# Modulation rows in 32-column strips, an eleventh leading block, and stores on another queue, in an adaLN + spectral mixer + MLP kernel

## The chip, the cores and the metric

One core of a Trainium2 chip runs the whole program in one launch. The metric is the device time of one execution in microseconds (us). Engines are named as in the profile: PE (TensorE, the matrix engine; PEld is its weight load), DVE (VectorE), ACT (ScalarE), POOL (GpSimd) and SP (SyncE, here only a queue that issues DMAs). An engine works through its own instructions in one order, which is fixed when the program is built.

## The reference

The reference is a forward pass and its vector-Jacobian product: the output, and the gradients of ten inputs (`out_1` to `out_9` after the output `out_0`; `B_x` is held constant). Cut to what matters:

```python
mod = (silu(c) @ w_mod).reshape(1, 6, 1, 1024)      # six rows: sa, ca, ga, sb, cb, gb
h = layernorm(x) * (1 + ca) + sa
x = x + ga * irfft2(rfft2(h) * (w_r + 1j * w_i))     # 2048 tokens x 1024
h = layernorm(x) * (1 + cb) + sb
x = x + gb * (gelu(layernorm(h) @ w1 + b1) @ w2 + b2)   # w1 1024x3584, w2 3584x1024
out, vjp = jax.vjp(f, A_x, A_w_r, A_w_i, B_w1, B_b1, B_w2, B_b2, c, w_mod)
return out, *vjp(grad_out)
```

The six modulation rows each need a product of one row of 1024 values with 1024x1024 weights. `out_9` is the gradient of `w_mod`: the outer product of silu(c) with the six row gradients, 1024x6144 values in bfloat16.

## The kernel before

Data are bfloat16, sums float32 in PSUM. Tokens are handled in four blocks of 512 (`NB`), the 3584 hidden columns in 28 blocks of 128 (`NFC`). The stages, in order of time:

1. *Start* (0 to 122 us). Modulation rows, layer norm of x, the turned gradient `gBoT` = (gb * grad_out)^T, and the products `ph = w2^T gBoT`, one block of 128 hidden columns at a time (`ph_part`: for each of four token blocks `j` a sum of eight matmuls into a PSUM tile of the pool "f", which has four buffers). `ph_out` casts each sum into one of four `phs` slots and, at the fourth, stores the slot to `d_ph` from POOL's queue. Beside this DVE scales and folds the normed x (`fold_d`, `fold_pair`, `fold_tok`) into `fbuf`.
2. *Spectral stage* (`spectral_core`, from `s_fwd` on), the transforms as products with cosine and sine matrices, then `consume_fwd` for each token block: residual, two layer norms, and the normed rows `n3`. The `ph` blocks that were not computed at the start are written behind it in the program, and fill PE where it waits.
3. *MLP*: `z_block` (product with w1, then GELU and its derivative on ACT and DVE) and `bo_pass` (product with w2), in the order of the list `plan`. The GELU buffers `gts` alternate between two sets, so a z block's casts wait for the product `hh` of the block two before it.
4. *Backward*: gradients through w1, the layer norms and the spectral part, with the products of the w2 gradient (`gw2_product`) and the w1 gradient (`pieces`, `gw1_quads`) handed out one at a time by `fill`.

*The modulation rows.* `u_b` holds silu(c) with each value repeated over 128 columns, so a product with a weight block gives the row already repeated in all 128 partitions. `mod_block(r, h)` does one half row (512 columns): one 1 MB load (`mod_load`) from SP's queue, eight matmuls, and a cast into its place by `nc.any` (the builder chooses DVE or ACT). The weight tiles `wblk` come from a ring of three buffers. Rows 5 and 1 come first; row 0 (two halves) stands behind block 3, and rows 2, 3 and 4 (six halves, three each) behind blocks 5 and 7. Row 0 is then multiplied by 8 and folded; 1 is added to rows 1 and 4.

*The order.* `ordered()` keeps a matmul behind the PE instruction written before it; `tc.issue_after(ins)` does the same for another engine. `tc.high_priority()` marks an instruction as urgent, which lets the builder put it ahead of others that are ready. `PH_EARLY = 10` says that blocks 0 to 10 are computed at the start; `load_w2t(fc)` loads a transposed w2 block into a ring of four, and `load_w1` starts the w1 loads at block 14 and block 27.

*The gradient of w_mod.* For rows 4, 2, 1 and 0 the last stage runs two generators beside the last products: `gmod_chain` (DVE: loads of `w_mod`, a product and a sum) and `gmod_scaled`, 32 scalings on ACT of a broadcast row `gr` into a ring of five buffers `gw`, each stored by a 256 KB DMA from POOL's queue. The loop at the end of the kernel draws one scaling per piece of the w1 gradient, and two for each of the last nine pieces. The last pieces are `gw1_quads`, four rounds of seven sums in which ACT copies ("snap") a partial sum out of PSUM before the next product is added to it:

```python
        for _ in range(2 if n >= left - 9 else 1):
            next(scaled, None)
```

Of the kernel before, what the change touches and what calls it, by code (L numbers as in the profile page):

```python
# [14 lines left out]
ALU = mybir.AluOpType  # L15
AX = mybir.AxisListType

P = 128
S = 2048
D = 1024  # L20
F = 3584
NT = S // P
NDC = D // P
NFC = F // P
KH = D // 2
# [10 lines left out]
def kernel(  # L36
# [24 lines left out]
    nc = tc.nc  # L61
# [11 lines left out]
    def ps_s(name):  # L73
        return psum.tile([P, 512], FP32, tag="s", name=name)
# [7 lines left out]
    ones_bf = const.tile([P, P], BF16, name="ones_bf")  # L82
# [168 lines left out]
    sarx = reg.tile([P, 3 * D], BF16, name="sar", tag="gm")  # L251
    sar = sarx[:, 0:2 * D].rearrange("p (a c d) -> p a c d", a=2, c=1)
# [5 lines left out]
    u_b = small.tile([P, NDC, P], BF16, name="u_b", tag="gmrow", bufs=1)  # L258
# [3 lines left out]
    sb_row, saf = sb_saf[:, 0, :], sb_saf[:, 1, :]  # L262
    MOD_DST = {0: sar[:, 0, 0, :], 1: opca_row, 2: ga_row, 3: sb_row, 4: opcb_row, 5: gb_row}
    wring = [0]

    def mod_tile():
        wring[0] += 1
        return reg.tile([P, NDC, KH], BF16, name="wblk", tag=PXT[3 + wring[0] % 3])

    def mod_load(r, h, wblk, eng, parts=1):  # L270
        cb = 2 * r + h
        src = w_mod[:, cb * KH:(cb + 1) * KH].rearrange("(j p) n -> p j n", p=P)
        for k in range(parts):
            js = slice(k * NDC // parts, (k + 1) * NDC // parts)
            eng.dma_start(out=wblk[:, js, :], in_=src[:, js, :])

    def mod_block(r, h, wblk=None):
        if wblk is None:
            wblk = mod_tile()[:]
            mod_load(r, h, wblk, nc.sync)  # L280
        pm = (ps_s, ps_d)[wring[0] % 2]("pm")
        for jc in range(NDC):
            nc.tensor.matmul(pm[:], lhsT=u_b[:, jc, :], rhs=wblk[:, jc, :], start=(jc == 0), stop=(jc == NDC - 1))
        dst = MOD_DST[r][:, h * KH:(h + 1) * KH]
        with tc.high_priority():
            nc.any.tensor_copy(out=dst, in_=pm[:])
        if r in (1, 4):
            nc.vector.tensor_scalar(out=dst, in0=dst, scalar1=1.0, scalar2=None, op0=ALU.add)

    def fold_d(dst, src, tmp):  # L290
        n = src.shape[1]
        fwd = src.rearrange("p c (b w) -> p c b w", w=512)[:, :, :, 0:256]
        rev = bass.AP(tensor=src.tensor, offset=src.offset + 1023, ap=[src.ap[0], [D, n], [-512, 2], [-1, 256]])
        tv = tmp.rearrange("p c (s b w) -> p c s b w", s=2, w=256)
        tt(tv[:, :, 0], fwd, rev, ALU.add)
        tt(tv[:, :, 1], fwd, rev, ALU.subtract)
        dv = dst.rearrange("p c (a b w) -> p c a b w", b=2, w=256)
        tt(dv[:, :, :, 0, :], tv[:, :, :, 0, :], tv[:, :, :, 1, :], ALU.add)
        return tt(dv[:, :, :, 1, :], tv[:, :, :, 0, :], tv[:, :, :, 1, :], ALU.subtract)
# [226 lines left out]
    last_pe = [None]  # L526

    def ordered():
        return tc.issue_after(last_pe[0].ins)

    PH_EARLY, PH_KEEP = 10, NFC - 4

    def ph_out(fc, j, pp):
        ph2 = phs[fc % 4]
# [9 lines left out]
    def ph_part(fc, js):  # L544
        for j in js:
            pp = ps_f("pp")
            for cch in range(NDC):
                last_pe[0] = nc.tensor.matmul(pp[:], lhsT=wt[:, fc % 4, cch, :], rhs=gBoT[j][:, cch, :],  # L548
                                              start=(cch == 0), stop=(cch == NDC - 1))
            ph_out(fc, j, pp)  # L550
# [24 lines left out]
    for j in range(4):  # L575
        n = 0
# [351 lines left out]

    phs.append(reg.tile([P, 4, BW], BF16, name="phr", tag="ph")[:])

    late_mods = [(r, h) for r in (2, 3, 4) for h in range(2)]
    for fc in range(PH_EARLY):
        if fc > 1:
            ph_part(fc, (0, 1, 2, 3))
        load_w2t(fc + 4)
        if fc == 4:
            with ordered():
                small_rows()
        if fc == 3:
            for h in range(2):  # L940
                with ordered():
                    mod_block(0, h)
            nc.vector.tensor_scalar(out=sar[:, 0], in0=sar[:, 0], scalar1=8.0, scalar2=None, op0=ALU.mult)
            fold_d(saf.rearrange("p (c d) -> p c d", c=1), sar[:, 0], sar[:, 1])
        if fc in (5, 7):
            with ordered():
                for r, h in late_mods[3 * (fc // 2 - 2):3 * (fc // 2 - 1)]:
                    mod_block(r, h)

    ph_part(PH_EARLY, (0, 1, 2, 3))  # L950
    early_pe = last_pe[0]
# [51 lines left out]
    def load_w1(n):  # L1003
        for _ in range(n):
            g = len(w1s)
            wtile = reg.tile([P, NDC, BW], BF16, name=f"w1_{g}", tag=W1T[g])
            with tc.issue_after(w2t_in[0].ins):
                w1_in.append(nc.sync.dma_start(out=wtile[:], in_=w1_v[:, :, g * BW:(g + 1) * BW]))
            w1s.append(wtile)
# [3 lines left out]
    for fc in range(PH_EARLY + 1, NFC):  # L1013
        if fc >= PH_EARLY + 4:
            load_w2t(fc)
            load_w1({14: 2, 27: 5}.get(fc, 0))
        if fc == N3_AT:
            n3Ts = [reg.tile([P, NDC, BW], BF16, name="n3Ta", tag="uv3")]
        for js in ((0, 1), (2, 3)) if fc < PH_KEEP else ((0, 1),):
            ph_part(fc, js)  # L1020
            if n3Ts and n3_turned[0] < NDC:
                cch = n3_turned[0]
                n3_turned[0] += 1
                pt = (ps_s, ps_d)[cch % 2]("pn")
                for q in range(4):
                    with ordered():
                        last_pn = nc.tensor.matmul(pt[:, q * P:(q + 1) * P], lhsT=n3h[0][:, q, cch * P:(cch + 1) * P], rhs=ident,
                                                   start=True, stop=True)
                last_pe[0] = last_pn
                with tc.high_priority():  # L1030
                    (s_copy, dve_copy)[cch % 2](n3Ts[0][:, cch, :], pt[:])
# [261 lines left out]
    def gmod_scaled(rows):  # L1293
        for n in range(len(rows) * NDC):
            k, jc = n // NDC, n % NDC
            gw, r = w1g["gw"][n % 5], rows[k]
            with tc.issue_after(w1g["ev"].ins):
                nc.scalar.activation(out=gw, in_=w1g["gr"][k], func=ACT.Identity, scale=u_rt[:, jc:jc + 1])
            nc.gpsimd.dma_start(out=out_9[jc * P:(jc + 1) * P, r * D:(r + 1) * D], in_=gw)
            yield  # L1300

    step_in = []
# [556 lines left out]
    for n in range(left):  # L1859
        fill(1)  # L1860
        k = [(32 - CHAIN_EARLY) * min(max(n + 17 + j - left, 0), 14) // 14 for j in range(2)]
        for _ in range(k[1] - k[0]):
            with tc.issue_after(w1g["dve"].ins):
                next(chain)
        for _ in range(2 if n >= left - 9 else 1):
            next(scaled, None)
    fin2 = reg.tile([P, 2, P], BF16, name="fin2", tag="ph")
    make_identity(nc, fin2[:, 0, :])
# [41 lines left out]
```

## Time and profile before

| | |
|---|---|
| median of 3 runs | 1374.16 us (1373.96 to 1374.2) |
| profiled execution | 1372.29 us |
| span of its profile, first to last instruction | 1370.3 us |
| granted TensorE clock, mean | 0.997 |
| PE, DVE, ACT, POOL busy | 98%, 79%, 58%, 28% of the span |
| DMA | 330 MB, 241 GB/s on the mean |

How to read the rows that follow. A timeline row is: start, duration (us), engine, line of the kernel, operation, output<-inputs by the program's names, tile and shape, and xN for N instructions merged; in brackets the idle time of the engine just before, and what released it. Durations of merged rows overlap at their ends, so the cost of a group is read from its start to the next group's start. A window row is: stretch, its length, then busy us of PE, PEld, DVE, ACT and POOL (instructions in brackets), granted clock, busy share of the DMA engines, GB/s. In a wait row stand the total, the number of times and the longest.

### The profile page before, as it was taken

What the parts mean: (1) busy time and instruction counts of PE and PEld (TensorE: products, weight loads), DVE (VectorE), ACT (ScalarE), POOL (GpSimd) and SP (SyncE); (2) the same over time, 40 slices, a digit from 0 to 9 for tenths busy, and PEclk for the clock granted to TensorE, in tenths of its full rate; (3) what the DMA queues carried; (4) which work ended last, traced back from release to release, by engine and by line L of the source; (5) the groups of instructions that cost most, each with busy time, mean ns of one, the idle gap of its engine ahead of it and who ended that gap; (6) DMA issues with size and microseconds to landing.
All of it is one profiled execution on the core that took longest, in us unless ns stands there. A gap on an engine that the chain in (4) does not pass through costs nothing. (4 is left out here: it accounts for less than half of the span.)

```text
span 1370.3 us, 18631 instructions
## 1 busy us (share of the span) xinstructions
PE 1345.6 (98%) x6899; PEld 651.0 (48%) x6899; DVE 1077.2 (79%) x1467; ACT 792.4 (58%) x1120; POOL 390.3 (28%) x436
## 2 busy tenths in 40 slices
PE   7999999999999999999999999999999999999997
PEld 4445566444444444444444444444644555444443
DVE  6997889999988878787620578889888488976985
ACT  4864667767877765665414593445732554544456
POOL 6273642411112122212211010112344330332163
PEclk9999999999999999999999999999999999999999
DMA  9975594899787887698999699988579878899876
GB/s 326 322 196 140 160 256 154 250 279 318 262 254 252 212 261 246 199 289 233 284 278 224 181 217 311 296 254 257 179 238 270 222 160 237 207 245 251 201 271 244
DMA packets 356401, 330.08 MB, mean 241 GB/s; under 512 B 203866, under 2 KB 298736, under 8 KB 356182
## 3 DMA queue, kind: packets, MB, share of 16 engines
q1 hardware_dynamic: 314310, 201.02, 57.2%
q0 software_dynamic: 35232, 120.00, 26.0%
q10 hardware_dynamic: 6768, 7.87, 1.7%
q8 instruction: 54, 0.88, 0.3%
q14 instruction: 37, 0.30, 0.1%
HBM read 165.73 MB, written 114.87 MB: 205 GB/s over the span
## 5 line engine op out<-in xcount | busy, mean ns | idle before, releaser
L1230 PE MATMUL pg<-w1T,gzr 128*128 128x512 bf16 x896 | 195.8, 380 | 0.0
L548 PE MATMUL pp<-gBoT,wt 128*128 128x512 bf16 x832 | 185.4, 379 | 3.2 <-ACT pho L540 1.9
L1076 PEld LDWEIGHTS <-w 128*128 128x128 bf16 x896 | 87.2, 98 | 107.4 <-issue 2.9
L1230 PEld LDWEIGHTS <-gzr 128*128 128x128 bf16 x896 | 86.5, 98 | 108.5 <-issue 5.8
L548 PEld LDWEIGHTS <-wt 128*128 128x128 bf16 x832 | 81.0, 98 | 97.9 <-issue 5.3
L1770 PE MATMUL gw1acc<-gzh,n3n 128*128 128x512 bf16 x512 | 111.8, 380 | 0.0
L1076 PE MATMUL pz<-n3Ta,w 128*128 128x512 bf16 x448 | 98.8, 380 | 1.4 <-ACT gt L1079 1.4
L1076 PE MATMUL pz<-n3Tb,w 128*128 128x512 bf16 x448 | 99.0, 380 | 0.0
L1770 PEld LDWEIGHTS <-n3n 128*128 128x128 bf16 x640 | 62.3, 98 | 76.7 <-issue 3.1
L195 DVE TENSOR_TENSOR ct<-ct 128x2048 bf16<-128x2048 bf16 (+1 forms) x84 | 91.5, 1120 | 4.3 <-ACT n L514 2.0
L1079 ACT ACTIVATE gt<-pz,b_col 128x512 bf16<-128x512 f32 x112 | 72.8, 682 | 37.3 <-PE pz L1076 33.1
L1130 PEld LDWEIGHTS <-hhA 128*128 128x128 bf16 x608 | 58.9, 98 | 73.2 <-issue 3.0
L1087 ACT ACTIVATE gt<-gt 128x2048 bf16<-128x2048 bf16 x28 | 53.5, 1911 | 58.3 <-DVE gt L195 58.3
L1411 PE MATMUL gw2acc<-gB,hhsA 128*128 128x512 bf16 x384 | 84.8, 380 | 0.0
L195 DVE TENSOR_TENSOR gt<-gt,gt 128x2048 bf16<-128x2048 bf16 x56 | 68.4, 1223 | 17.7 <-ACT gt L1089 16.8
L1419 ACT CAST gwo<-gw2acc 128x512 bf16<-128x512 f32 x40 | 23.5, 588 | 87.5 <-PE gw2acc L1411 84.2
L1411 PEld LDWEIGHTS <-hhsA 128*128 128x128 bf16 x384 | 37.5, 98 | 43.5
L1083 ACT ACTIVATE gt<-gt 128x2048 bf16<-128x2048 bf16 x28 | 53.4, 1908 | 3.1 <-DVE hhC L195 2.4
L540 ACT CAST pho<-pp 128x512 bf16<-128x512 f32 x68 | 38.6, 584 | 27.3 <-PE pp L548 24.1
L1774 ACT CAST gwo<-gw1acc 128x512 bf16<-128x512 f32 x40 | 23.0, 579 | 53.6 <-PE gw1acc L1770 41.6
L1089 ACT ACTIVATE gt<-gt 128x2048 bf16<-128x2048 bf16 x28 | 53.3, 1905 | 0.3
L1411 PE MATMUL gw2acc<-gB,otl 128*128 128x512 bf16 x224 | 50.0, 380 | 0.0
(414 smaller groups left out, 2710.3 us busy)
## 6 DMA issues: line engine op xcount, KB each, us to landing
gzr<-d_gz SPq DMA_DIRECT2D x28, 512.0 KB
d_ph<-pho POOLq DMA_DIRECT2D x21, 512.0 KB, 5.5
wblk<-in_w_mod_dram SPq DMA_DIRECT2D x10, 1024.0 KB
out_dram<-otl POOLq DMA_DIRECT2D x40, 256.0 KB, 4.1
d_hh<-hhA POOLq DMA_DIRECT2D x19, 512.0 KB, 5.6
wrw<-in_w_mod_dram SPq DMA_DIRECT2D x32, 256.0 KB
w<-in_B_w_dram SPq DMA_DIRECT2D x7, 1024.0 KB
hhC<-d_ph SPq DMA_DIRECT2D x14, 512.0 KB
```

The lines of the kernel that those rows point to most:

```text
L195: return nc.vector.tensor_tensor(out=out, in0=a, in1=b, op=op)
L540: copy(out=ov, in_=pv)
L548: last_pe[0] = nc.tensor.matmul(pp[:], lhsT=wt[:, fc % 4, cch, :], rhs=gBoT[j][:, cch, :], start=(cch == 0), stop=(cch == NDC - 1))
L1076: last_pe[0] = nc.tensor.matmul(pz[:], lhsT=w1s[g][:, cch, k * P:(k + 1) * P], rhs=n3T[:, cch, :], start=(cch == 0), stop=(cch == NDC - 1))
L1079: z_in = nc.scalar.activation(out=zb[:, k, :], in_=pz[:], func=ACT.Identity, bias=b1_col[:, fc:fc + 1], scale=1.0)
L1083: nc.scalar.activation(out=av, in_=zb, func=ACT.Square)
L1087: nc.scalar.activation(out=sg, in_=bv, func=ACT.Sigmoid, scale=2.0 * GK)
L1089: nc.scalar.activation(out=bv, in_=bv, func=ACT.Sigmoid, scale=-2.0 * GK)
L1130: last_pe[0] = nc.tensor.matmul(pbs[i][:], lhsT=hh[:, k, i * P:(i + 1) * P], rhs=wp[:, k, :], start=False, stop=(g == 6 and k == 3))
L1230: last_pg[0] = nc.tensor.matmul(pgs[i][:], lhsT=gzs[b, g][:, k, i * P:(i + 1) * P], rhs=w1Ts[g][:, k, h * KH:(h + 1) * KH], start=(g == 0 ...
L1411: nc.tensor.matmul(acc[:], lhsT=hh_of(fc)[:, t, :], rhs=gBs[t // 4][:, t % 4, h * KH:(h + 1) * KH], start=(t == 0), stop=(t == NT - 1))
L1770: nc.tensor.matmul(acc[:], lhsT=n3ns[t // 4][:, t % 4, cch * P:(cch + 1) * P], rhs=gz2[t // 8][:, t % 8, :], start=(t == 0), stop=(t == NT ...
```

## The change

There are three parts.

- *Strips.* The eight half rows of rows 0, 2, 3 and 4 are no longer done by `mod_block` but in groups of two, three and three by `mod_strips`. It loads all blocks of its group, and runs for each of the eight chunks `jc` one matmul per half row with 32 columns of `u_b`, each into its own 32 partitions of one PSUM tile. ACT casts these strips to `strips` (a part of `sarx` that is free). The function `spread` that it returns is called later, between the first two and the last two token blocks of the next `ph` block: a matmul with one row of ones and one row of the strip repeats each half row over all partitions, and ACT casts it into its place. The multiplication by 8, the fold of row 0 and the addition of 1 to row 4 move into `spread`.
- *Leading blocks.* `PH_EARLY` goes from 10 to 11, so blocks 0 to 11 stand ahead of the spectral stage and the filler has one block less; the first w1 loads are keyed to block 15, the first that still loads.
- *Stores.* `gmod_scaled` stores from ACT's queue, and the loop at the end draws two scalings per piece from the start.

```diff
+    strips = sarx[:, 2 * D + KH:3 * D]
+
+    def mod_strips(rows):
+        wblks = []
+        for r, h in rows:
+            wblks.append(mod_tile()[:])
+            mod_load(r, h, wblks[-1], nc.sync)
+        pm = ps_s("pm")
+        for jc in range(NDC):
+            for k in range(len(rows)):
+                with ordered():
+                    last_pe[0] = nc.tensor.matmul(pm[32 * k:32 * (k + 1), :], lhsT=u_b[:, jc, 0:32], rhs=wblks[k][:, jc, :],
+                                                  start=(jc == 0), stop=(jc == NDC - 1))
+        n = 32 * len(rows)
+        with tc.high_priority():
+            nc.scalar.copy(out=strips[0:n, :], in_=pm[0:n, :])
+
+        def spread():
+            for k, (r, h) in enumerate(rows):
+                pr = (ps_d, ps_s)[k % 2]("pr")
+                with ordered():
+                    last_pe[0] = nc.tensor.matmul(pr[:], lhsT=ones_bf[32 * k:32 * k + 1, :], rhs=strips[32 * k:32 * k + 1, :],
+                                                  start=True, stop=True, tile_position=(32 * k, 0))
+                dst = MOD_DST[r][:, h * KH:(h + 1) * KH]
+                with tc.high_priority():
+                    nc.scalar.copy(out=dst, in_=pr[:])
+                if r == 4:
+                    nc.vector.tensor_scalar(out=dst, in0=dst, scalar1=1.0, scalar2=None, op0=ALU.add)
+            if rows[0][0] == 0:
+                nc.vector.tensor_scalar(out=sar[:, 0], in0=sar[:, 0], scalar1=8.0, scalar2=None, op0=ALU.mult)
+                fold_d(saf.rearrange("p (c d) -> p c d", c=1), sar[:, 0], sar[:, 1])
+        return spread
...
-    PH_EARLY, PH_KEEP = 10, NFC - 4
+    PH_EARLY, PH_KEEP = 11, NFC - 4
...
+    spread = None
     for fc in range(PH_EARLY):
         if fc > 1:
-            ph_part(fc, (0, 1, 2, 3))
+            ph_part(fc, (0, 1))
+            if spread is not None:
+                spread = spread()
+            ph_part(fc, (2, 3))
         load_w2t(fc + 4)
...
         if fc == 3:
-            for h in range(2):
-                with ordered():
-                    mod_block(0, h)
-            nc.vector.tensor_scalar(out=sar[:, 0], in0=sar[:, 0], scalar1=8.0, scalar2=None, op0=ALU.mult)
-            fold_d(saf.rearrange("p (c d) -> p c d", c=1), sar[:, 0], sar[:, 1])
+            spread = mod_strips([(0, 0), (0, 1)])
         if fc in (5, 7):
-            with ordered():
-                for r, h in late_mods[3 * (fc // 2 - 2):3 * (fc // 2 - 1)]:
-                    mod_block(r, h)
+            spread = mod_strips(late_mods[3 * (fc // 2 - 2):3 * (fc // 2 - 1)])
...
-            load_w1({14: 2, 27: 5}.get(fc, 0))
+            load_w1({15: 2, 27: 5}.get(fc, 0))
...
-            nc.gpsimd.dma_start(out=out_9[jc * P:(jc + 1) * P, r * D:(r + 1) * D], in_=gw)
+            nc.scalar.dma_start(out=out_9[jc * P:(jc + 1) * P, r * D:(r + 1) * D], in_=gw)
...
-        for _ in range(2 if n >= left - 9 else 1):
+        for _ in range(2):
             next(scaled, None)
```

## Prediction

> **What bounds the kernel now.** I read the page's busy line first, then TensorE's waits, a window of the middle, the chain that ended last, and then the timelines of the places that the change touches. TensorE (PE) is busy for 98% of the span and its named waits are short.
>
> ```profile
> PE 1345.6 (98%) x6899; PEld 651.0 (48%) x6899; DVE 1077.2 (79%) x1467; ACT 792.4 (58%) x1120; POOL 390.3 (28%) x436
> ```
> ```profile
> PE pm L283 <- DMA wblk<-in_w_mod_dram: 2.8, 1, 2.8
> ...
> PE pz L1076 <- ACT gt L1079: 1.4, 1, 1.4
> ```
> ```profile
> 341.00:1286.00 945.00, 942.73 (x4711) 443.26 (x4711) 716.69 (x917) 514.87 (x693) 210.56 (x238) 1.00 0.89 241
> ```
> ```profile
> 1286.72 27.79 PE gw1acc L1770 x128
> ...
> 1363.14 0.58 ACT gwo L1676
> ```
>
> A wait row gives line, what was waited for, total us, times, longest. The window row (length, then busy PE, PEld, DVE, ACT, POOL) shows that from 341 to 1286 us TensorE stands still for only 945.00 - 942.73 = 2.3 us while VectorE (DVE) is busy for 717 of 945. So what TensorE reaches earlier at 341 us should arrive at the end of the span. The question is whether work taken off TensorE before 341 us lets it pass 341 us earlier. That stretch has to be read on VectorE:
>
> ```profile
> 206.00:264.00 58.00, 58.00 (x337) 32.68 (x336) 57.65 (x73) 44.09 (x78) 19.93 (x15) 1.00 0.56 188
> ```
> ```profile
> 330.00:340.00 10.00, 9.53 (x45) 4.20 (x43) 10.00 (x16) 6.51 (x7) 3.65 (x3) 1.00 1.08 276
> ```
> ```profile
> 304.01 7.07 PE L1076 MATMUL pz<-n3Ta,w 128*128 128x512 bf16 x32
> ...
> 340.98 7.07 PE L1076 MATMUL pz<-n3Ta,w 128*128 128x512 bf16 x32 [1.44 <-ACT gt L1079]
> ```
> ```profile
> 340.24 2.42 ACT L1079 ACTIVATE gt<-pz,b_col 128x512 bf16<-128x512 f32 x4 [3.69 <-DVE hhB L195]
> ```
> ```profile
> 322.71 0.17 DVE L501 TENSOR_SCALAR mv<-mv 128x2 f32<-128x2 f32 x1 [2.92 <-ACT ct L500]
> ...
> 338.94 1.21 DVE L195 TENSOR_TENSOR hhB<-gt,gt 128x2048 bf16<-128x2048 bf16 x1
> ```
>
> VectorE works 57.65 of 58 us from 206 on and all of 330 to 340; it has one hole of 2.92 us that ends at 322.71. At 340.98 TensorE's fourth z block waits for ScalarE (ACT), which had waited 3.69 us for `hhB`, the GELU product of the first z block. That block left TensorE at 311 us; its product was made 28 us later, behind layer-norm work. So here TensorE is no earlier than VectorE lets it be, and the w2^T blocks (`ph_part`) fill its time.
>
> **The change part by part.** *The strips.* Removed are eight `mod_block`s, 64 matmuls, which stand in the timeline as a group of 16 and two of 24:
>
> ```profile
> 56.56 3.62 PE L283 MATMUL pm<-wblk,u_b 128*128 128x512 bf16 x16
> 60.01 7.07 PE L548 MATMUL pp<-gBoT,wt 128*128 128x512 bf16 x32
> ...
> 75.07 5.34 PE L283 MATMUL pm<-wblk,u_b 128*128 128x512 bf16 x24
> 80.25 12.25 PE L548 MATMUL pp<-gBoT,wt 128*128 128x512 bf16 x56
> ...
> 95.97 5.34 PE L283 MATMUL pm<-wblk,u_b 128*128 128x512 bf16 x24
> 101.14 20.88 PE L548 MATMUL pp<-gBoT,wt 128*128 128x512 bf16 x96
> 121.86 1.04 PE L639 MATMUL pu<-smax,fbuf 128*128 128x256 bf16 x8
> ```
>
> From each start to the next group's start: 3.45 + 5.18 + 5.17 = 13.80 us. Added are as many matmuls of 32 columns, two or three strips at a time, and eight one-row matmuls. Both shapes run elsewhere in the trace:
>
> ```profile
> 773.58 0.61 PE L218 MATMUL acc3a<-gn3a,ones_bf 128*32 128x512 bf16 x4
> 774.12 2.12 PE L1230 MATMUL pg<-w1T,gzr 128*128 128x512 bf16 x9
> ```
> ```profile
> 783.51 1.04 PE L218 MATMUL acc3a<-pru,ones_bf 128*32 128x512 bf16 x8
> 784.48 3.84 PE L1230 MATMUL pg<-w1T,gzr 128*128 128x512 bf16 x17
> ```
> ```profile
> 347.98 0.40 PE L1119 MATMUL pbo<-b_row,ones_bf 1*128 1x512 bf16 x4
> 348.30 3.63 PE L1130 MATMUL pbo<-w2sA,hhB 128*128 128x512 bf16 x16
> ```
>
> Four strip matmuls, in pairs, take 0.54 us to the next group and eight take 0.97: a pair costs (0.97 - 0.54) / 2 = 0.215, going in and out 0.11. A group of the change is eight such steps, 8 x 0.215 + 0.11 = 1.83; three are 5.5 us. Four one-row matmuls take 0.32 us, so three spreads take at most 0.96. TensorE saves 13.80 - 5.5 - 0.96 = 7.3 us. Bounds: strips that did not overlap would cost what the blocks cost, and with the spreads the part would lose 1.3 us; spreads at 0.215 would make it 7.7. I take 7.3, as the pair rows have the same shape.
>
> The Trainium skill speaks against this: TensorEngine Tiling (Array Packing), Tiling Modes, says that a change of tiling mode drains TensorE, and here there are twelve changes. An estimate by that rule, with a pipeline tail of 0.380 - 0.215 = 0.165 us for each, leaves 13.80 - 3 x 1.72 - 0.96 - 2.0 = 5.7 us instead of 7.3. The 0.11 us for going in and out together is less than one such tail, so I keep 7.3.
>
> What the strips wait for: a group starts when all its blocks are loaded and frees their slots together, so the third group's 3 MB are issued about 14 us (two blocks of 6.9) ahead of their use. I cost that at nothing: the two blocks hide it; without them the nearest row is the 2.8 us that a product once waited for `wblk`. A spread waits for the cast of its strips on ScalarE, which half a block (3.45 us) covers; the casts to the rows move to ScalarE too, at 0.58 us each (the length of the cast in the chain above), eleven casts, 6.4 us, where TensorE then already runs the next half. Uncovered, one cast is 0.58 us for each spread, 1.7 us.
>
> *Eleven leading blocks.* One `ph_part`, 6.9 us, goes from the filler behind 122 us to before the spectral stage. That stage then starts at 121.86 - 7.34 + 6.90 = 121.4, 0.4 us earlier, and its last input is ready:
>
> ```profile
> 118.54 0.69 DVE L195 TENSOR_TENSOR fbuf<-fbuf,sb_saf 128x1024 bf16<-128x1024 bf16 x1
> ```
> ```profile
> 118.69 1.07 ACT L540 CAST pho<-pp 128x512 bf16<-128x512 f32 x2 [2.95 <-DMA d_ph<-pho]
> ```
>
> The z blocks come 7.3 us earlier on TensorE, but VectorE's layer norms move only by the 0.4. What it gives: the first z block's GELU can use the hole of 2.92 us, and what stands behind it on VectorE moves up as much. Lower end 0 (VectorE's order stays), upper end the rest of 7.3 (the products move ahead of the layer norms). I take 2.9, the idle time that is there. The moved block's transpose, its `d_ph` store on GpSimd (POOL) and the w1 loads now keyed to block 15 pass SP and POOL ahead of work that is due 20 us later: nothing; without that, a z block would wait like the 1.4 us row above.
>
> *Stores of out_9 from ScalarE, two scalings per step.* From 1286.72 on TensorE runs without a gap and the span ends with its last product, a cast and a store on SP, none of them touched. There is nothing to gain, only to lose:
>
> ```profile
> L1298 ACT ACTIVATE otl<-gr,u_rt x32: 1134/1148/1162, 1291.3 to 1361.3; 128x1024 bf16<-128x1024 bf16 x32
> ```
> ```profile
> L1421 ACTq DMA_DIRECT2D out_dram<-gwo x36: 338/338/398, 997.4 to 1166.4; - x36
> ```
> ```profile
> 1334.06 5.30 ACT L1298 ACTIVATE otl<-gr,u_rt 128x1024 bf16<-128x1024 bf16 x5
> 1339.27 0.57 ACT L1668 COPY snap<-gqy 128x512 f32<-128x512 f32 x1
> ```
>
> Five scalings take 5.3 us now, 1.06 each; with a store of 0.34 behind each it is up to 1.15 + 0.34 = 1.49. A store that waits for its scaling holds the snapshots behind it on ScalarE, and TensorE's next sum into that buffer waits for the snapshot. A round of the quad products (seven sums of eight matmuls, each 27.79 / 128 = 0.217 us by the chain above: 12.1 us) has four casts of 0.58 and now eight scalings: 2.3 + 11.9 = 14.2 us, 2.1 more than the round, over two rounds 4.2. Bounds 0 and 4.2. I take 0: the snapshots are marked urgent, and the two later rounds then have no scalings, so late scalings have room there. The 32 store issues leave POOL's queue, which nobody on the path waits for.
>
> *Sum*: -0.4 - 2.9 + 0 = -3.3 us of the 7.3 saved. The profiled execution took 1372.29 us (span 1370.3 and 2.0 around it), so 1369.0 for its like; the median 1374.16 stands 1.9 above it, and against that I predict 1370.9.
>
> **The rivals.** *All of it survives.* The z blocks' GELU is placed ahead of the third and fourth layer norm, which are not needed so early. For it: VectorE has 945 - 717 us free later. Against: `hhB` stood behind layer norms for the whole of 330 to 340. 1374.2 - 7.3 = 1366.9.
>
> *Nothing survives.* VectorE's order stays, TensorE waits at the fourth z block for 1.44 + 6.9 us. For it: VectorE is full. Against: the hole. 1374.2 - 0.4 = 1373.8.
>
> *The leading blocks are held, slower.* Four `ph` slots are emptied by POOL; now block ten's casts could not start before 118.69, when a `d_ph` store had landed. If TensorE reaches block ten at 107.7, its four results fill the PSUM buffers by 114.6 and block eleven waits until about 119.3; the spectral stage starts at 119.3 + 6.9 = 126.2, 4.3 us later, VectorE's chain with it, and there is 7.3 us less filler to use the time: 1374.2 + 4.3 = 1378.5. It decides once that store lands later than 114.6. Against: the store's block is also computed 4 us or more earlier, and may be issued before POOL is held up. What POOL waited for then is a 128x2 scaling that took 17.48 us while VectorE ran without a pause:
>
> ```profile
> 93.81 17.48 POOL L615 TENSOR_SCALAR em<-em 128x2 bf16<-128x2 bf16 x1 [8.63 <-ACT em L614]
> ```
>
> *ScalarE holds the quad products.* 4.2 us lost there against 3.3 gained: 1374.2 + 0.9 = 1375.1.
>
> **How the numbers follow.** About 0.2% (2.7 us) is what a measurement of this kernel can tell from no change. Forecast 0.38, its own range 1369 to 1372.5 (from some 5 to 1.7 us gained); all survives 0.17; nothing 0.17; blocks held 0.18; ScalarE 0.10. Faster: 0.17 and three quarters of the forecast, 0.29, is 0.46; slower: the held blocks and a part of the ScalarE case where nothing survives in front, 0.23; the same: 0.31. The range reaches from the full case (1366.5) to the held blocks (1378.5).
>
> **What would show it.** Right: `mod` groups of 1.8 us and spreads of 0.3; the first spectral product near 121.4; z blocks from about 297; a wait of some 5 us at the fourth z block, which then starts near 337.7; no gap behind 1284. Wrong: a spectral start near 126, a fourth z block without a wait (full) or one at 340.5 (nothing), or TensorE waits at `gqy` and `gqw`.

## The result and the profile after

The changed kernel takes 1391.89 us (median of 6 runs, 1388.14 to 1399.37), the kernel before on the same chip 1374.18 (6 runs, 1372.58 to 1377.64). The ratio is 1.0131, 95% interval 1.0101 to 1.0162: 17.7 us slower, where 3.3 us faster was predicted. The profiled execution took 1393.06 us with a span of 1391.2; before it was 1372.29 and 1370.3.

The page's busy line of the changed kernel, and the longest of TensorE's waits (line, what was waited for, total us, times, longest):

```profile
PE 1338.2 (96%) x6780; PEld 648.7 (47%) x6907; DVE 1078.0 (77%) x1468; ACT 797.6 (57%) x1124; POOL 358.3 (26%) x404
```
```profile
PE pz L1107 <- ACT gt L1110: 10.3, 3, 8.1
PE pm L301 <- DMA wblk<-in_w_mod_dram: 6.4, 1, 6.4
PE gqy L1717 <- ACT snap L1699: 4.4, 1, 4.4
```

The 1338.2 us are not to be set against the 1345.6 of before. The trace of the changed kernel has 6780 matmuls beside 6907 weight loads, so 127 matmul records are missing, and each missing one reads as some 0.05 us of idle time; a second profile of the kernel before (below), which lacks 128, reads 1337.4. (So a z block of 32 matmuls reads x31 below.) What the strips save is read from their groups. TensorE's longest waits are at three places: the third group of strips, the z blocks, and the quad products. The first row that follows is of the kernel before; then comes TensorE's timeline of the changed kernel at the strips, the spectral stage, the fifth z block (z block 0, group 4) and the quads:

```profile
39.29 3.62 PE L283 MATMUL pm<-wblk,u_b 128*128 128x512 bf16 x16
```
```profile
44.33 3.62 PE L283 MATMUL pm<-wblk,u_b 128*128 128x512 bf16 x16
61.69 1.90 PE L301 MATMUL pm<-wblk,u_b 128*32 128x512 bf16 x16
...
79.35 1.91 PE L301 MATMUL pm<-wblk,u_b 128*32 128x512 bf16 x24
81.19 3.63 PE L581 MATMUL pp<-gBoT,wt 128*128 128x512 bf16 x15
...
95.54 0.81 PE L301 MATMUL pm<-wblk,u_b 128*32 128x512 bf16 x2
102.75 3.19 PE L301 MATMUL pm<-wblk,u_b 128*32 128x512 bf16 x22 [6.41 <-DMA wblk<-in_w_mod_dram]
105.87 3.63 PE L581 MATMUL pp<-gBoT,wt 128*128 128x512 bf16 x16
...
133.94 1.04 PE L672 MATMUL pu<-smax,fbuf 128*128 128x256 bf16 x8
...
364.63 8.84 PE L1107 MATMUL pz<-n3Ta,w 128*128 128x512 bf16 x31 [8.11 <-ACT gt L1110]
...
1340.27 2.84 PE L1717 MATMUL gqy<-gzh,ct 128*128 128x512 bf16 x8 [4.44 <-ACT snap L1699]
```

The first product over the later `w_mod` loads, in code that the change leaves alone, comes 5.0 us later than before (44.33 against 39.29), so this pair of executions is not a fair one to subtract. A second profile of each program gives a better pair (`e10_before_again`, then `e12_after_again`; their expectations are further down):

```profile
42.25 3.62 PE L283 MATMUL pm<-wblk,u_b 128*128 128x512 bf16 x16
122.81 1.04 PE L639 MATMUL pu<-smax,fbuf 128*128 128x256 bf16 x8
305.04 7.07 PE L1076 MATMUL pz<-n3Ta,w 128*128 128x512 bf16 x32
1316.67 1.89 PE L1686 MATMUL gqy<-gzu,n3n 128*128 128x512 bf16 x7
```
```profile
42.12 3.62 PE L283 MATMUL pm<-wblk,u_b 128*128 128x512 bf16 x16
98.96 3.42 PE L301 MATMUL pm<-wblk,u_b 128*32 128x512 bf16 x22 [5.49 <-DMA wblk<-in_w_mod_dram]
130.38 1.04 PE L672 MATMUL pu<-smax,fbuf 128*128 128x256 bf16 x8
305.15 7.07 PE L1107 MATMUL pz<-n3Ta,w 128*128 128x512 bf16 x31
361.00 8.98 PE L1107 MATMUL pz<-n3Ta,w 128*128 128x512 bf16 x31 [8.10 <-ACT gt L1110]
1332.27 1.44 PE L1717 MATMUL gqy<-gzu,n3n 128*128 128x512 bf16 x3 [5.23 <-ACT gwo L1805]
1340.76 3.25 PE L1717 MATMUL gqy<-gzh,ct 128*128 128x512 bf16 x8 [2.20 <-ACT snap L1699]
```

Both start alike (42.25 and 42.12). The changed kernel is 7.6 us late at the spectral stage, level again at the first z block (one block less of filler), and 15.6 us late at the quads. TensorE's last product ends at 1387.8 against 1365.5 us, 22.3 late, and the span ends at 1391.7 against 1372.7: the end of the kernel gives 3.3 us back.

### The profile page after: what moved, and what is told of

It reads as the page before. It is cut to its first block, busy times and chain, and to the rows that moved or that the text cites. A ratio compares the mean times of both kernels' runs of the same rounds, so it can differ in the third digit from the quotient of the medians.

```text
span 1391.2 us, 18500 instructions
## 1 busy us (share of the span) xinstructions
PE 1338.2 (96%) x6780; PEld 648.7 (47%) x6907; DVE 1078.0 (77%) x1468; ACT 797.6 (57%) x1124; POOL 358.3 (26%) x404
## 5 line engine op out<-in xcount | busy, mean ns | idle before, releaser
L1107 PE MATMUL pz<-n3Ta,w 128*128 128x512 bf16 x437 | 99.7, 384 | 10.8 <-ACT gt L1110 10.3
L1110 ACT ACTIVATE gt<-pz,b_col 128x512 bf16<-128x512 f32 x112 | 73.1, 685 | 41.6 <-PE pz L1107 36.9
L1118 ACT ACTIVATE gt<-gt 128x2048 bf16<-128x2048 bf16 x28 | 53.5, 1910 | 55.5 <-DVE gt L195 55.5
```

The costliest lines, as they stand in the source:

```text
L1107: last_pe[0] = nc.tensor.matmul(pz[:], lhsT=w1s[g][:, cch, k * P:(k + 1) * P], rhs=n3T[:, cch, :], start=(cch == 0), stop=(cch == NDC - 1))
L1110: z_in = nc.scalar.activation(out=zb[:, k, :], in_=pz[:], func=ACT.Identity, bias=b1_col[:, fc:fc + 1], scale=1.0)
L1118: nc.scalar.activation(out=sg, in_=bv, func=ACT.Sigmoid, scale=2.0 * GK)
```

## Experiments

Every kernel computes the whole reference. Ratios are to the kernel before, run on the same chip in the same session, with 95% intervals.

### One part at a time

`e1_front_only` is the changed kernel with its last two hunks undone (stores and pace):

```
-            nc.scalar.dma_start(out=out_9[...], in_=gw)
+            nc.gpsimd.dma_start(out=out_9[...], in_=gw)
-        for _ in range(2):
+        for _ in range(2 if n >= left - 9 else 1):
```

> The changed kernel with its third part undone (scalings stored from GpSimd's queue again, one a step and two in the last nine). Theory A (two separate costs: the front, which is group 3's wait for its weight blocks of 6.4 us, the moved w2^T block of 6.9 us and the late VectorE chain behind them; and the quad products held up by ScalarE, +6.5 us, less a tail that is 3.3 us shorter): about 14.5 us slower than before, 1388 to 1389 us, a TensorE wait of 6 us at the pm strips of line 301 and of about 8 us at pz, and quads as long as before (46.7 us). Rival B (ScalarE's stores are the whole cost): within 3 us of before, 1374 to 1377 us. Rival C (the first 5 us, where TensorE waits for fbuf and wblk in code that the change leaves alone, are part of the difference): the mod(1,h) group starts near 44 us again.

`e2_stores_only` is the kernel before with just these two hunks.

> The kernel before with the third part alone (scalings stored from ScalarE's queue, two a step from the start). Theory A: quads 53 us instead of 46.7 with a wait of 4 us at gqy, TensorE's end to the span's end 3.9 us instead of 7.2, so +6.5 - 3.3 = about 3 us slower, 1377 us. Rival B (the quads are late in the changed kernel only because what comes before is): 3.3 us faster, 1371 us. Rival C (ScalarE's stores are the whole cost of the change): about 17 us slower, 1391 us.

`e3_group3_late` is the changed kernel with `if fc in (5, 9)` for `if fc in (5, 7)` (and the slice of rows to match), so that the third group stands after block 9.

> The changed kernel with the third group of strips two blocks later (after block 9 instead of 7, spread in block 10), so that its three 3 MB loads have 14 us more. Theory A: no wait at the third group, spectral start 126 us instead of 134, the wait at pz of z block 0, group 4 shrinks by the same 8 us, 1382 to 1384 us. Rival D (the VectorE chain is late for another reason than the spectral start, such as the rows that the third group gives): the wait at pz stays near 8 us and the time within 2 us of the changed kernel's 1391.9.

`e4_block_only` is the kernel before with `PH_EARLY = 11` and `{15: 2, 27: 5}`.

> The kernel before with eleven leading blocks (and the w1 loads one block later) and nothing else. Theory A (the start of the spectral part sets VectorE's chain, which had 1.2 us to spare at z block 0, group 4): spectral start 128.8 us, a wait of 5 to 6 us at that group and slow matmuls of 1 to 2 us behind it, 6 to 8 us slower, 1380 to 1382 us. Rival D (a moved block costs nothing, since the filler is a block shorter): 1374 us.

Measured: e1 1386.27 us against 1372.67 (1.0093, 1.0077 to 1.0110); e2 1381.79 (1.0058, 1.0036 to 1.0079); e3 1385.27 (1.0097, 1.0076 to 1.0118); e4 1389.03 (1.0125, 1.0101 to 1.0149). Both halves of the change cost time by themselves: 13.6 us for the front, near theory A's 14.5, and 9.1 us for the stores, which is three times theory A's 3 (in e1 mod(1,h) began at 42.1 us, so the start is no large part of it). Together that is 22.7 us, 5 more than the whole change cost; why the parts don't add up is open. The profiled executions of e1 and e2 were the slowest of theirs. In e2 TensorE waits at the quads for ScalarE:

```profile
PE gqy L1686 <- ACT gwo L1774: 5.0, 1, 5.0
...
PE gqy L1686 <- ACT snap L1668: 2.6, 1, 2.6
```

e3's third group did not wait; so 14 us were too little for the loads (three of 1 MB each). But the wait at the z blocks did not shrink by 8 us, as I had expected it to with an earlier spectral stage. TensorE's total waits at `pz`, in e3, e4 and (below) e15:

```profile
PE pz L1110 <- ACT gt L1113: 9.3, 3, 8.1
```
```profile
PE pz L1076 <- ACT gt L1079: 10.1, 3, 8.1
```
```profile
PE pz L1076 <- ACT gt L1079: 18.3, 3, 9.6
```

The longest wait is 8.1 us in every kernel with eleven leading blocks, with strips or without, and wherever the spectral stage starts (e1's row reads 10.2 us in all, with 8.1 as the longest). Before, the row read 1.4 us. Start times of three products on TensorE, in brackets counted from the first spectral product; the fifth z block (z block 0, group 4) is the one that waits 8.1 us:

| | leading blocks | first spectral product | first z block | fifth z block |
|---|---|---|---|---|
| e10, the kernel before | 10 | 122.81 | 305.04 (182.2) | 352.80 (230.0) |
| e12, the changed kernel | 11 | 130.38 | 305.15 (174.8) | 361.00 (230.6) |
| e3 | 11 | 126.16 | 300.93 (174.8) | 356.77 (230.6) |
| e4 | 11 | 129.40 | 304.21 (174.8) | 360.06 (230.7) |
| e15 | 12 | 140.34 | 310.96 (170.6) | 375.76 (235.4) |

So the fifth z block is timed from the start of the spectral stage, by a chain of layer norms on VectorE and ScalarE, and the filler behind that stage is the cover of the chain: with a block less of it the z blocks come 7.4 us sooner after the stage's start, and the fifth does not. Theory A of e3 had the wrong reason, since an earlier spectral stage brings the z blocks forward as much as the chain. That of e4 had the right one, with a wait (5 to 6 us) and a time (1380 to 1382 us) that were too small.

`e15_block12` is the kernel before with twelve (`{16: 2, 27: 5}`).

> The kernel before with twelve leading blocks. Theory A (each block taken out of the filler uncovers its 6.9 us): the wait at z block 0, group 4 is 8.1 + 6.9 = 15.0 us, the spectral stage starts near 136 to 139 us, and the time is some 7 us above that with eleven, 1394 to 1398 us. Rival F (the 8.1 us are a fixed order of ScalarE's instructions): 8.1 us again, and the time stays near 1389 us.

It took 1398.3 us in its one execution, and the `pz` waits are 18.3 us: 1.4, 10.1 and 18.3 us with ten, eleven and twelve blocks, so 8.7 and 8.2 us more for each block of 6.9 us. With twelve they are spread over two z blocks, 6.9 and 9.6 us, where theory A had one wait of 15.0; rival F's unchanged 8.1 us falls. How the wait comes about stands in ScalarE's and VectorE's timelines of the changed kernel; the first row is ScalarE's before, at the same casts:

```profile
349.89 2.40 ACT L1079 ACTIVATE gt<-pz,b_col 128x512 bf16<-128x512 f32 x4
```
```profile
360.30 1.91 ACT L1118 ACTIVATE gt<-gt 128x2048 bf16<-128x2048 bf16 x1 [8.76 <-DVE gt L195]
...
363.91 2.40 ACT L1110 ACTIVATE gt<-pz,b_col 128x512 bf16<-128x512 f32 x4
```
```profile
341.99 0.18 DVE L508 RECIPROCAL stats<-mv 128x4 f32<-128x4 f32 x1 [4.90 <-ACT mv L506]
...
345.40 2.29 DVE L195 TENSOR_TENSOR ct<-ct,rows 128x4096 bf16<-128x4096 bf16 x1 [2.00 <-ACT ct L547]
...
351.07 1.87 DVE L516 BATCH_NORM_STATS2 st<-ct 128x6 f32<-128x512 bf16 x3
...
359.04 1.22 DVE L195 TENSOR_TENSOR gt<-gt 128x2048 bf16<-128x2048 bf16 x1
```

ScalarE's Sigmoid (L1118) needs a GELU product that VectorE makes at 359.04, after the last chunk's norm statistics that began at 351.07. The copies that empty TensorE's `pz` buffers (L1110, at 363.91) stand behind that Sigmoid on ScalarE, so TensorE stops too.

Not all of the wait is missing cover. VectorE isn't full on the way: it stands still for 4.90 and 2.00 us until ScalarE is done with a square root and a norm, where before it had stood still for 2.92. ScalarE now does the first z block's Sigmoid (331.60), four passes of a norm, four casts and a table load ahead of that square root (341.65); before, it did the square root as soon as its input was there (322.91) and the Sigmoid behind it (328.59). Counted from the first spectral product, the last norm statistics begin 5.0 us later than before (217.1 against 212.1), and the casts at `pz` 1.9 us (230.0 against 228.0). No run tried another order on ScalarE.

### The strips without the block

`e5_strips10_late` is the strips with ten blocks, the third group late, stores and pace as before; `e6_strips10` has the third group after block 7.

> The strips alone: ten leading blocks as before, the third group after block 9, scalings stored from GpSimd's queue and paced as before. Theory A (the filler behind the spectral stage is cover for VectorE's layer norm of the last chunk: a block moved out of it comes back as a wait of 8.1 us, whenever the spectral stage starts): with ten blocks no wait of 8 us at z block 0, group 4. The spectral stage then waits for VectorE's last fold, which ended 2.8 us ahead of it in the run with eleven blocks and the late group, so that TensorE, 6.9 us earlier, idles some 4 us there; 2 to 3 us faster than before, 1370 to 1371 us. Rival E (nothing else binds): the whole 7.3 us, 1365 to 1366 us. Rival F (the wait at z block 0 comes from the strips' casts on ScalarE and not from the block): the wait of 8.1 us is there again and the time is 1380 us or more.

> The same with the third group after block 7, where the change has it. Theory A: its loads still come about 5 to 6 us late, but the spectral stage has to wait for VectorE's last fold anyway, so most of that is hidden: 1371 to 1375 us. Rival G (the late loads cost their full wait and the slow matmuls behind it, 7 to 8 us, wherever they stand): 1378 us or more.

e5: 1378.62 us against 1372.73 (1.0031, 1.0010 to 1.0051; its ten runs go from 1371.9 to 1387.9). e6: 1382.76 (1.0076, 1.0054 to 1.0099). With ten blocks the 8.1 us are gone from both (the `pz` waits are 2.9 and 4.1 us in all), so rival F falls. The expected wait for VectorE is there in e5:

```profile
121.44 1.67 PE L672 MATMUL pu<-smax,fbuf 128*128 128x256 bf16 x7 [4.33 <-DVE fbuf L195]
```

The time was not as expected: 4 us slower than before by the ratio, not 2 to 3 faster. The profiled execution, the slowest of its runs, lost more in waits of 2.6, 2.4 and 4.1 us between 370 and 990 us that the kernel before did not have, and in slow matmuls behind them; what the median lost is open. In e6 the third group waited 4.3 us again; its time is rival G's, not theory A's, so the late loads were not hidden behind the wait for VectorE.

`e11_casts_act` adds to e5 one edit in `ph_out`, which takes the casts of the leading blocks' results off VectorE:

```
-        copy = nc.any.tensor_copy if fc <= PH_EARLY else ...
+        copy = nc.any.tensor_copy if fc < 4 else ...
```

> The strips alone (ten leading blocks, third group late) with the casts of the leading blocks' results from block 4 on all on ScalarE, where before they were shared out between ScalarE and VectorE (0.67 us each on VectorE). Theory A (with strips TensorE is early enough, and the spectral stage waits 4.3 us for VectorE's last fold): VectorE does up to 12 casts, 8 us, less by then; the fold is done 4 us or more earlier, TensorE's wait of 4.3 us there goes to 0 to 1, and the time is 4 to 6 us below the strips alone, 1368 to 1375 us. Rival H (VectorE waits for ScalarE's norms there, which the casts delay): the wait stays at 4 us or grows, and so does the time.

1370.73 us against 1373.48 (0.9980, 0.9964 to 0.9997). VectorE's last fold in e5, then in e11, and TensorE's first two spectral products in e11:

```profile
120.69 0.68 DVE L195 TENSOR_TENSOR fbuf<-fbuf,sb_saf 128x1024 bf16<-128x1024 bf16 x1
```
```profile
118.03 0.69 DVE L195 TENSOR_TENSOR fbuf<-fbuf,sb_saf 128x1024 bf16<-128x1024 bf16 x1
```
```profile
118.43 1.29 PE L672 MATMUL pu<-smax,fbuf 128*128 128x256 bf16 x8
121.94 1.03 PE L672 MATMUL pu<-smax,fbuf 128*128 128x256 bf16 x8 [1.79 <-DVE U L936]
```

The fold is 2.7 us earlier (theory A: 4 or more), the first product no longer waits, and a wait of 1.8 us before the next took the place of 4.3. So strips and casts together bring 2.7 us by the medians: with VectorE relieved ahead of the spectral stage, TensorE's earlier arrival no longer ends in front of VectorE there. The casts without the strips were not run, so how much of the 2.7 us is theirs alone is open.

### The stores

`e7_act_old_pace` is the kernel before with stores from ScalarE's queue at the old pace; `e8_pool_two` is two scalings a step, stored from GpSimd's queue.

> The kernel before with the scalings stored from ScalarE's queue but paced as before (one a step, two in the last nine). Theory A (a store on ScalarE's queue has to wait for a transfer of SyncE's queue that it has no data from, since both take turns on the same completion counters: with two a step the eighth store waited 11 us for the store of row 0 of d_gmod, and all casts behind it on ScalarE too): with one a step ScalarE comes to that store 7 to 10 us later, so a wait of 0 to 4 us and quads 0 to 3 us longer; 1373 to 1377 us. Rival B (the issue of 0.34 us for each store is what ScalarE lacks): quads 5 to 6 us longer as with two a step, 1379 us or more.

> The kernel before with two scalings a step from the start, stored from GpSimd's queue. Theory A: no wait of 11 us for the row of d_gmod behind the stores; the quads within 2 us of before, and the stretch from TensorE's last sum to the span's end shorter by up to 3 us, since no scaling's store is left for the end: 1370 to 1374 us. Rival B (eight scalings a round are too many for ScalarE, whatever stores them): quads 4 to 6 us longer, 1377 us or more.

e7: 1383.57 us (1.0081, 1.0062 to 1.0100). e8: 1383.17 (1.0082, 1.0052 to 1.0111). Both numbers are those of rival B, but neither mechanism is. ScalarE's longest waits for a DMA from 1280 us on, in e2, e7 and e8 (its one long wait for VectorE, 9.4 to 12.9 us in these runs, is there in the kernel before too, with 11.7):

```profile
ACT otl L1298 <- DMA d_gmod<-row: 11.7, 1, 11.7
```
```profile
ACT gwo L1774 <- DMA d_gmod<-row: 6.9, 1, 6.9
```
```profile
ACT otl L1298 <- DMA out_dram<-otl: 16.4, 2, 14.2
```

In e2 and e7 a store on ScalarE's queue waits until SyncE's store of row 0 of `d_gmod` has landed. The two have no data in common, but in the traces the transfers of both queues report to the same eight completion counters, in turn. In e2 row 0's store, issued at 1320.68, and the ScalarE store that is issued behind it, at 1321.86, report to the same one; so the second waits until the first has landed. SyncE's transfer itself was waiting for VectorE. The changed kernel shows it on both queues:

```profile
1318.66 10.43 ACTq L1330 DMA_DIRECT2D out_dram<-otl  x2
1329.14 2.19 ACT L1329 ACTIVATE otl<-gr,u_rt 128x1024 bf16<-128x1024 bf16 x2 [9.95 <-DMA d_gmod<-row]
```
```profile
1314.55 0.35 SPq L1310 DMA_DIRECT2D gr<-d_gmod  x1
1327.56 0.22 SPq L201 DMA_DIRECT2D d_gmod<-row  x1
```

SyncE issues nothing from 1314.9 to 1327.56; 1.6 us later ScalarE goes on. In e8 it is GpSimd's queue that is held, by scatters that wait for VectorE, and the scalings run out of their five slots:

```profile
1300.08 6.81 POOL L167 DMA_INDIRECT out_dram<-ct,xu  x1 [10.47 <-DVE ct L195]
```

`e9_row0_gpsimd` is e2 with row 0's store moved to GpSimd's queue (`(nc.sync if r else nc.gpsimd).dma_start` in `store_gmod`).

> The kernel before with the third part (stores from ScalarE's queue, two scalings a step) and one more edit: the store of row 0 of d_gmod, for which ScalarE's eighth store waited 11.7 us, goes to GpSimd's queue instead of SyncE's. Theory A (ScalarE's store waited for SyncE's transfer): the wait of 7 to 12 us for d_gmod on ScalarE is gone, TensorE does not wait 5 us at the quads' start, and the stretch behind TensorE's last sum stays short: 1370 to 1374 us. Rival B (two scalings a step and their issues are too much for ScalarE): the waits at gqy stay and the time is that of the third part alone, 1380 to 1383 us.

1382.16 us (1.0064, 1.0038 to 1.0089); theory A's time was wrong. Its ten runs go from 1376.26 to 1392.55, and the profiled one is the fastest. There the wait for row 0 is gone, but its place went to the next load that SyncE held for VectorE:

```profile
ACT otl L1298 <- DMA wrw<-in_w_mod_dram: 11.0, 1, 11.0
```

That supports the dependence on SyncE's queue (another transfer of it, as long a wait), and says that moving one transfer doesn't remove it. Not run were the stores on ScalarE's queue at the later pace that follows, which would tell what their issues cost without such a wait.

`e14_pace` is the kernel before with `range(2 if n >= 8 else 1)`: two scalings a step, but only from the ninth step on, which is meant to be after these queues are free. `e13_best` is e11 with the same pace.

> The kernel before with that pace alone. Theory A: 3.3 us faster by the shorter end, 1369 to 1371 us, quads 46.7 us long. Rival B: quads 3 to 6 us longer, 1373 to 1377 us.

> The strips with ten leading blocks, the late third group and the casts on ScalarE, and with scalings stored from GpSimd's queue, one a step in the first eight steps and two from then on, so that they end three steps before the last. Theory A (the shorter end of the changed kernel comes from scalings that are done early, and the waits of 11 to 14 us from scalings that come before SyncE's and GpSimd's queues are free): the end 3.3 us shorter, no new wait at the quads, 1366 to 1369 us, 4 to 7 us below the kernel before. Rival B (two scalings a step hold the quad products whenever they come): quads 3 to 6 us longer, 1370 to 1374 us.

e14: 1370.43 us against 1375.9 (0.9975, 0.9953 to 0.9997). e13: 1366.05 us against 1375.9 (0.9930, 0.9903 to 0.9958), the fastest kernel of the study, some 10 us below the kernel before and, across sessions, 26 below the changed one. Both times are those of theory A, but the gains of 5.5 and 9.9 us by the medians are larger than its 3.3 and 4 to 7, and the kernel before ran 1.7 to 3.2 us slower here than in the other sessions; nor was e13 quite free of waits at the quads (1.9 us at `gqy`). From TensorE's last product to the span's end it is 3.5 us in e13 and e14, as in e8 (3.5) and the changed kernel (3.9); it is 7.2 us before and in e11, and 8.9 in e7 (each the span less the end of the last product), whose stores go out from ScalarE at the old pace. So the shorter end comes from scalings that are done early, not from the queue. The last GpSimd store, before and then in e14:

```profile
1362.75 0.54 POOL L1299 DMA_DIRECT2D out_dram<-otl  x1 [0.49 <-ACT otl L1298]
```
```profile
1354.13 0.54 POOL L1299 DMA_DIRECT2D out_dram<-otl  x1 [0.86 <-ACT otl L1298]
```

### The same programs once more

> The kernel before once more, for a second profile of the same program. If the start (the first products over w_mod at 39.3 us, while the changed kernel's were at 44.3) varies from run to run with the loads, mod(1,h) begins anywhere from 39 to 44 us and the time moves with it by as much; if it belongs to the program, it begins at 39.3 again. From 700 to 970 us TensorE had no wait before and up to 6 us in the other kernels: the same question.

> The changed kernel once more, for a second profile: the waits that belong to the program (6.4 us for the third group's blocks, 8.1 us at z block 0, group 4, 4.4 us at the quads) should come again within 1 us, and what does not come again, at the start or between 700 and 970 us, is variation from run to run.

The kernel before took 1374.69 us, the changed one 1393.59. The rows are above. mod(1,h) began at 39.3 and 42.2 us in the one program, at 44.3 and 42.1 in the other, so 2 to 3 us of the start vary from run to run. The three waits came back: 5.5 us for the blocks, 8.1 at the z block, and 5.2 + 2.2 at the quads, where one of 4.4 had stood; the last is not within the 1 us that was expected. From 700 to 970 us the second profile of before has a wait of 2.4 us at `pg` that the first lacks.

## Why the prediction was wrong, step by step

- *The strips' saving (7.3 us)* was right. Group two took 1.84 us (79.35 to 81.19) against 1.83, the three spreads took 0.32 us each, and a spread waited 0.8 us at most for its cast in the first profile (2.6 in e1).
- *"I cost that at nothing: the two blocks hide it"* failed. From 95.54 to 105.87 the third group took 10.3 us instead of 1.83 (6.4 of it waiting); in the second profile the wait was 5.5. The loads of three blocks, whose buffers group two frees together at 81.19, were all in at 102.75, 21.6 us later, and I had priced 14 as enough without a row for three such loads at once. The nearest row, 2.8 us, was no bound: it was one wait of another load. There was a nearer one. SyncE's issues of the three loads, before and then in the changed kernel:

```profile
76.99 3.82 SPq L275 DMA_DIRECT2D wblk<-in_w_mod_dram  x3
```
```profile
82.14 5.18 SPq L275 DMA_DIRECT2D wblk<-in_w_mod_dram  x3
```

Before, the first load had 19.0 us until its product (95.97), and the other blocks were needed one after the other behind it. Strips need all three within their first three matmuls, 13.4 us after the first issue. Two blocks were there; only the third was late (two matmuls ran at 95.54, the rest from 102.75). The DMA engines' busy share reads 1.05 from 82.0 to 95.5 us and 1.23 from there to 102.7, so other transfers were under way; which of them held the third block is open.

- *"That stage then starts at 121.4"* failed by this alone. In the pair with equal starts it came at 130.38 against 122.81, +7.6: the -0.4 of the prediction and 8.1 us for the third group. It was near neither 121.4 nor the 126.2 of the rival that holds the blocks, whose `d_ph` wait did not show.
- *The gain of 2.9 us from VectorE's hole* failed. The hole was not used but grew, to 4.90 + 2.00 us, since VectorE waits in it for ScalarE, whose order had changed. (It was not VectorE's one hole either: two of 1.81 and 1.97 us end at 271.58 and 288.77 before.) The rival "nothing survives", with 1.44 + 6.9 us of waiting, has nearly the right size: the `pz` waits rose from 1.4 to 10.3 us. The place was one block off: the fourth z block waited 0.74 us, the fifth 8.1. I counted TensorE's earlier arrival at the z blocks as a possible gain, but the fifth starts 230.6 us after the spectral stage, whenever TensorE is ready. So the block that was moved ahead of that stage takes back there what the strips had saved, and what it no longer covers behind the stage is waiting. Without the third group's wait the fifth z block would have started at 121.4 + 230.6 = 352.0 us, an estimate from these rows; before it started at 351.77, so there was nothing to gain. I had also left out that TensorE comes back slow: a z block of 32 matmuls (31 in the trace) took 8.84 and 8.98 us, where 7.07 is usual, 1.8 to 1.9 us more.
- *"I take 0" for ScalarE's stores* failed, and so did its upper bound of 4.2 us: the part alone cost 9.1 us. The bound came from ScalarE's busy time (scalings and issues of 0.34 us). The cost was a wait: 10 to 12 us behind SyncE's queue. I had asked what leaves GpSimd's queue, and not what ScalarE's shares with SyncE's.
- *"There is nothing to gain" at the end* failed the other way: 3.3 us came back (3.9 us instead of 7.2), by the pace. I had the span end with TensorE's last product, a cast and a store of SyncE; but the scalings' last store left GpSimd at 1362.75, as late as that product.

The sum over the pair with equal starts: the front gives +10.4 us up to the backward spectral stage at 970 us (8.7 more waiting at `pz`, 1.9 of slow matmuls, 1.2 of waiting at `pp` and 0.9 more at `pbo`, less the 2.4 us that the kernel before waited at `pg` in this execution), the stretch from there +11.9 (5.2 us of wait ahead of the quads and 6.7 in them, 2.2 of it waiting and most of the rest slow matmuls: the granted clock was 0.68 from 1332 to 1341 us and 0.81 from there to 1350), the end -3.3: 19.0 us between these two spans, 17.7 between the medians. Shown by experiment are the third group's wait (e3, by its trace; its ratio's interval overlaps that of the whole change), the cover (e4, e15, e5), the tie of ScalarE's stores to SyncE's transfers (e2, e7, e9) and the pace (e8, e14). Open are why e4, the block alone, cost 16.4 us by its median where the waits and slow matmuls of its profiled execution, the fastest of four, add up to 11; what part the order on ScalarE has in the 8.1 us; and what the median of e5 lost.

The Trainium skill, DMA: Bandwidth & Descriptors, Issuing engines are not separate DMA queues, says that issuing from several engines saves only the sequencer's time to initiate a transfer. The trace agrees that nothing was gained, and goes beyond it: with stores of 0.34 us each on ScalarE, ScalarE stood still for 6.9 to 11.7 us.

## To carry to other kernels

Work that fills an engine behind a long chain is the cover of that chain: moving a piece of it ahead of the chain's start makes the chain start later by the piece's length, and the engine then waits for it as long, since it has that much less to do meanwhile. The trace of before shows the margin (here 1.4 us of waiting at one block and none at the next). Before a store changes its queue, look for what that queue will wait for, not only for what the issue costs; a queue whose neighbour is held by a slow producer can be held with it. Before products are interleaved, look for when each one's load is due: what was needed one after the other is then needed at once. Price such loads by a row of the same number of bytes under way, not by the time that happens to be there until the first use.

## What the runs showed of the hardware

After a long wait TensorE's next matmuls are slow. The rows above give a z block in 8.84 us after 8.11; a wait of 2.9 us did it too, as this row of e6 shows, while a z block after 1.4 us took the usual 7.07. The granted clock shows it, in windows of the changed kernel from the fifth z block on (second fence); behind the strips' wait, from 102.70 to 110.00 us, it was 0.81:

```profile
346.04 8.55 PE L1107 MATMUL pz<-n3Ta,w 128*128 128x512 bf16 x32 [2.92 <-ACT gt L1110]
```
```profile
364.00:374.00 10.00, 9.32 (x35) 3.85 (x36) 7.94 (x12) 9.91 (x11) 0.52 (x1) 0.79 0.66 228
374.00:388.00 14.00, 13.23 (x61) 5.92 (x61) 13.73 (x14) 10.76 (x10) 2.50 (x4) 1.00 0.56 188
```

So a stall has a second price, and the clock is full again some 10 us on. Z blocks after waits of 2.6 to 9.6 us took 8.42 to 9.79 us in these runs, 1.4 to 2.7 more than usual. The length of the wait alone doesn't decide below 2.9 us: 2.6 us at 375.51 in e5 were followed by a clock of 0.75, but 2.8 us at 685.51 in e7 and 2.6 at 700.75 in the changed kernel by a full one. The Trainium skill, TensorE: Matmul & The Clock Gate, HAM oscillation, says that gaps of more than about 3.4 us bring the slow clock back; the traces agree for longer waits, and differ below: 2.9 us were enough in the row above, and 2.6 in e5, and the measurement decides.
